# Four key units of the second batch moved into the first batch's weight chain, and its values spread wider

## The chip, the core and the metric

One core of a Trainium2 chip runs the whole kernel. The metric is device microseconds of one execution. TensorE (PE) multiplies and transposes into PSUM, VectorE (DVE), ScalarE (ACT) and GpSimd (POOL) do the rest, and SyncE (SP) issues most of the DMAs from one queue, in order.

## What is computed

Agent attention over four batches of 11,456 tokens of width 128, with 49 agents a batch, and then a mixture of eight experts of which each token goes to one:

```python
a2k = sm(agents, k)              # 49 x 11456, softmax over the keys
agent_v = a2k @ v                # 49 x 128
x = (sm(q, agents) @ agent_v).reshape(B * S, D)
logits = xn @ en.T / tau         # xn, en: rows scaled to length one
expert_idx = np.argmax(logits, axis=1)
out[mask] = gate_w[mask, None] * (np.maximum(x[mask] @ w1[e], 0.0) @ w2[e])
```

## The kernel before

**Units and tiles.** A batch is cut into 12 units of 8 columns of 128 tokens (the last is short), and each unit into two tiles, 23 in all. A *key unit* (`("k", b, u)`) is loaded, transposed, multiplied with the batch's agents (`aT_all`) to 392 columns of scores, copied to SBUF (`s_u`), and taken into a running maximum (`m_run`). After the last, `k_max` makes the maximum over all keys. A *value unit* (`k2_unit`) takes the exponentials of a key unit's scores and multiplies them with the values. `av_chain` folds the sums into `avT`, the 49 agents' values, from which `pick_expert` finds the expert that most tokens of the batch will take, loads its weights (`w1s`, `w2s`), multiplies `avT` with `w1s` (`gp`), orders the hidden units by a key of each (`key`, spread over the partitions by the products `row`, ranked by L739 and L741), gathers the first 256 (`placed`, then `gh`, `gl`; `w2pp`, then `w2p`) and makes a linear remainder (`linp`, `lin`) and a test for tokens that need more (`vm`, `thr`). A *query unit* (`q_unit`) yields the attention weights `tt`, transposed, and then the tiles of the network: `hp`, `hh` and `hl`, `yp`, `ot`, with one store for each tile.

**Two ways for a key unit.** The first batch's go through `k1_f32`: eight 32-bit transposes on TensorE in two halves, one copied out by ScalarE and one by VectorE (`pe_T`), then eight 32-bit products, which the profile shows as 16, with 49 columns. For later batches the odd units do the same. The even ones (`k1_pairs`) are scaled and split into two 16-bit parts (L462, L466, L472), transposed by a DMA on SP's queue (`kT`, L477), and multiplied in 24 16-bit products (L486 to L488).

**Order.** The instructions are written by generators (`spawn`, `yield`) that a loop advances tick by tick: four ticks for each tile, 92 for a batch. A scheduler then orders each engine's queue from a timeline of its own; `in_place(x)` only says that what it encloses comes after `x` on that engine, and `tc.high_priority()` that it goes ahead where it can. In the profile each engine works through its queue in order.

**The stages.** `first()` writes the first batch's keys and values, and then, with nothing of the network to do yet, the chain of `av_chain(0, 0)` and `pick_expert`. TensorE's waits there are filled with products of a tile of zeros (`zero_products`: `ZV` in front of the fold, `ZG` in front of `gp`, `ZA` in front of `row`, `ZB` in front of `placed`). The third and fourth query units (`q_unit(0, 2)`, `q_unit(0, 3)`) are brought up beside it; lists such as `c_last`, `g_last`, `s_last` hold the last instruction of `gp`, of `row` and of the ranking, for `in_place`. After the chain, the first batch's tiles run beside the second batch's keys and values, which `plan()` asks for at fixed ticks: `W_` holds for each batch the shares of a batch at which keys begin and end and values begin and end. The loads go into a ring of `LB` = 10 buffers, in the order in which they are asked for; a load waits until the buffer ten before it has been used.

## Time and profile before

| what | value |
|---|---|
| median of 3 runs | 755.49 us (755.04 to 762.77) |
| the profiled execution | 765.48 us, of which 763.7 us span |
| mean granted TensorE clock | 0.949 |
| busy: TensorE, VectorE, ScalarE, GpSimd | 700.0, 586.5, 468.2, 347.1 us |
| DMA | 125.61 MB, 164 GB/s on the mean |

Busy times are unions over the span, and matmuls are pipelined with modelled ends, so a full TensorE is one that always has something in flight. The clock is a share of 2.4 GHz; 0.50 is the 1.2 GHz level.

### The profile page before, as it was taken

How to read it: one execution, taken by the hardware profiler on the slowest of the kernel's cores; microseconds unless marked ns; L12 is line 12 of the kernel's file. 1: busy time of each engine (PE TensorE's matmuls, PEld its weight loads, DVE VectorE, ACT ScalarE, POOL GpSimd, SP SyncE). 2: the span in 40 equal slices, each digit the busy share in tenths (PEclk: the TensorE clock that was granted, in tenths of full speed). 3: DMA queues.
4: the chain of work that ended last, by engine and by line, in shares of the span. 5: the costliest groups of instructions: out<-in, count | busy, mean ns of one | idle time of the engine just before them, and what ended most of it. 6: DMA issues, size and time to landing. Idle time of an engine off the chain costs nothing. (4 is left out here: it accounts for less than half of the span.)

```text
span 763.7 us, 20762 instructions
## 1 busy us (share of the span) xinstructions
PE 700.0 (92%) x7980; PEld 598.5 (78%) x7980; DVE 586.5 (77%) x1594; ACT 468.2 (61%) x1216; POOL 347.1 (45%) x605
## 2 busy tenths in 40 slices
PE   8998999879997989999999769999999989899996
PEld 7986789768887868778788658887888868777675
DVE  4654898758764898976578789897678799868993
ACT  3354577748663883477567566566656774469841
POOL 5000148236523551676361671547662763866500
PEclk9967899989998989999999879999999999999999
DMA  9935089996854953966795914957563742332321
GB/s 341 282 111 184 12 226 235 242 200 154 217 153 147 291 115 122 269 147 198 181 201 163 262 47 98 285 151 223 131 200 94 219 112 56 104 58 83 128 73 63
DMA packets 167285, 125.61 MB, mean 164 GB/s; under 512 B 87034, under 2 KB 143440, under 8 KB 167186
## 3 DMA queue, kind: packets, MB, share of 16 engines
q1 hardware_dynamic: 153746, 100.59, 52.3%
q10 hardware_dynamic: 13120, 23.47, 8.7%
q8 instruction: 63, 1.03, 0.6%
q14 instruction: 36, 0.29, 0.1%
q0 software_dynamic: 320, 0.23, 0.1%
HBM read 80.26 MB, written 23.79 MB: 136 GB/s over the span
## 5 line engine op out<-in xcount | busy, mean ns | idle before, releaser
L1157 ACT ACTIVATE hh<-hp 128x512 f16<-128x512 f32 (+1 forms) x184 | 106.9, 586 | 65.0 <-PE hp L1154 52.5
L1158 DVE SCALAR_TENSOR_TENSOR hl<-hp,hh 128x512 f16<-128x512 f32 (+1 forms) x184 | 122.4, 667 | 26.2 <-ACT hh L1157 25.4
L1181 PE MATMUL yp<-w2p,hh 128*128 128x128 f16 x720 | 138.6, 221 | 1.8 <-ACT hh L1157 1.6
L1182 PE MATMUL yp<-w2p,hh 128*128 128x128 f16 x720 | 138.8, 221 | 0.0
L1183 PE MATMUL yp<-w2p,hl 128*128 128x128 f16 x720 | 136.1, 221 | 0.9 <-DVE hl L1158 0.9
L1025 ACT ACTIVATE vp<-vp,la 128x320 f32<-128x320 f32 x224 | 112.0, 500 | 31.6 <-PE vp L1022 21.5
L1022 PE MATMUL vp<-vm,tt 128*128 128x320 f16 x360 | 98.5, 301 | 9.5 <-DVE vmin L1027 2.8
L869 PEld LDWEIGHTS sp<-aT_all,fT 128*128 128x128 f32 x720 | 90.1, 198 | 5.4 <-issue 1.6
L869 PE MATMUL sp<-aT_all,fT 128*128 128x49 f32 x720 | 92.1, 278 | 1.1 <-DVE qe L879 1.1
L1181 PEld LDWEIGHTS <-hh 128*128 128x128 f16 x720 | 72.8, 101 | 17.5 <-ACT hh L1157 6.2
L888 POOL TENSOR_TENSOR e<-qe,e 128x392 f16<-128x392 f32 (+1 forms) x46 | 41.4, 901 | 92.5 <-ACT e L887 81.4
L1183 PEld LDWEIGHTS <-hl 128*128 128x128 f16 x720 | 72.0, 100 | 10.4 <-issue 2.2
L1182 PEld LDWEIGHTS <-hh 128*128 128x128 f16 x720 | 71.6, 99 | 5.2
L1027 DVE TENSOR_REDUCE vmin<-vp 128x1 f32<-128x320 f32 (+1 forms) x136 | 64.7, 479 | 13.0 <-PE vp L1022 12.4
L1153 PE MATMUL hp<-tt,gh 128*128 128x512 f16 (+1 forms) x184 | 70.0, 382 | 2.5 <-DVE vmin L1027 1.0
L1154 PE MATMUL hp<-tt,gl 128*128 128x512 f16 (+1 forms) x184 | 69.8, 380 | 0.0
L972 POOL TENSOR_TENSOR nrm<-qq,half 128x16 f32<-128x16 f32 (+2 forms) x28 | 68.5, 2448 | 0.5
L1196 DVE TENSOR_TENSOR ot<-yp,gs 128x512 f32<-128x512 f32 (+1 forms) x92 | 61.4, 669 | 7.4 <-PE yp L1183 6.9
L1172 PE MATMUL yp<-lin,tt 128*128 128x128 f16 x720 | 64.6, 222 | 0.4
L420 DVE COPY fT<-fTp 128x512 f32<-128x512 f32 x68 | 46.2, 679 | 23.4 <-PE fTp L416 23.0
L423 ACT COPY fT<-fTp 128x512 f32<-128x512 f32 (+1 forms) x80 | 44.6, 559 | 30.0 <-PE fTp L416 20.2
L416 PE MATMUL fTp<-ident,qt 128*128 128x128 f32 (+1 forms) x344 | 55.0, 286 | 2.6 <-ACT vp L1025 1.6
(361 smaller groups left out, 1753.5 us busy)
## 6 DMA issues: line engine op xcount, KB each, us to landing
kt<-in_k_dram SPq DMA_DIRECT2D x44, 512.0 KB, 7.1
vt<-in_v_dram SPq DMA_DIRECT2D x44, 512.0 KB, 6.1
out_dram<-ot ACTq DMA_DIRECT2D x88, 256.0 KB, 3.0
qt<-in_q_dram SPq DMA_DIRECT2D x42, 512.0 KB, 5.2
w1s<-in_moe_w_dram SPq DMA_DIRECT2D x9, 512.0 KB, 3.6
w2s<-in_moe_w_dram SPq DMA_DIRECT2D x9, 512.0 KB, 5.5
q<-in_q_dram SPq DMA_DIRECT2D x2, 512.0 KB, 12.0
tt<-e SPq DMA_TRANSPOSE x46, 3.6
```

The lines of the kernel that those rows point to most:

```text
L869: i_ = pe.matmul(out=s[:p, c * A : (c + 1) * A], lhsT=xT[:, c * p : (c + 1) * p], rhs=aT_all[:, b, :], start=True, stop=True)
L972: pool.tensor_tensor(out=nrm, in0=quad, in1=half[:, :n], op=ALU.pow)
L1022: pe.matmul(out=z[:p, :FV], lhsT=tts[b, u][:, c * p : (c + 1) * p], rhs=bt.vm, start=True, stop=True)
L1025: act.activation(z[:p, :FV], z[:p, :FV], AF.Relu, bias=bt.l[:p, at], scale=-1.0, accum_out=bt.vsum[:p, at])
L1027: dve.tensor_reduce(out=bt.vmin[:p, at], in_=z[:p, :FV], axis=AX.X, op=ALU.min)
L1153: pe.matmul(out=hp[:, :m], lhsT=bt.gh[:, fs], rhs=tt, start=True, stop=False)
L1154: pe.matmul(out=hp[:, :m], lhsT=bt.gl[:, fs], rhs=tt, start=False, stop=True)
L1157: h_last[:] = [act.activation(hh[:, :m], hp[:, :m], AF.Relu)]
L1158: dve.scalar_tensor_tensor(out=hl[:, :m], in0=hp[:, :m], scalar=0.0, in1=hh[:, :m], op0=ALU.max, op1=ALU.subtract)
L1181: pe.matmul(out=y, lhsT=hh[:, cs], rhs=wh, start=False, stop=False, skip_group_check=True)
L1182: pe.matmul(out=y, lhsT=hh[:, cs], rhs=wl, start=False, stop=False, skip_group_check=True)
L1183: y_last[:] = [pe.matmul(out=y, lhsT=hl[:, cs], rhs=wh, start=False, stop=last, skip_group_check=True)]
```

## The change

Four key units of the second batch (`NEXT = 4`) are loaded while the first batch's values come free, and worked on in the first batch's chain, all four in 32 bits. Units 0 to 2 are transposed after the transpose in `av_chain` that ends it (`q_last`). The scores of units 0 and 1 and the transposes of unit 3 come after `gp`; the scores of units 2 and 3 come after `row`, and their copies after the ranking. The maxima of units 1 to 3 are taken on VectorE after the copy that makes `w2p`; unit 0's scores become the running maximum by a copy on GpSimd. Zero products in front of `gp` go from 8 to 2, those in front of `row` are left out, and those in front of `placed` go from 18 to 6. The third query unit's transposes come after the scores of unit 3. In the plan the other eight key units take 0 to 0.19 of a batch where twelve took 0 to 0.28, and the values 0.24 to 0.52.

```diff
--- before.py
+++ after.py
@@ -60,12 +60,13 @@
     LEAD = min(4, NU)
     LAG = 5
     HOLD = 2
+    NEXT = 4
     TB = 8
     XB = 3
     LB = 10
     XS = 2
     WARM = 9
-    ZV, ZG, ZA, ZB = 3, 8, 10, 18
+    ZV, ZG, ZB = 3, 2, 6
 
     groups = [[0]]
     while groups[-1][-1] < NU - 1:
@@ -377,6 +378,7 @@
 
     y_last, h_last, p_last, w_last = [], [], [], []
     k_T = {}
+    z_last, q_last = [], []
     a_last, f_last, n_last, c_last, v_last = [], [], [], [], []
     k_last, m_last, d_last, r_last, s_last, g_last = [], [], [], [], [], []
     h_slots = slots(XS)
@@ -415,7 +417,7 @@
                 for c in range(m):
                     pe.transpose(out=tp[:, c * p : (c + 1) * p], in_=src[:p, c0 + c, :], identity=ident[:p, :p])
             dst = xT[:, c0 * p : (c0 + m) * p]
-            if c0 and not both:
+            if (c0 and not both) or both is None:
                 with in_place(floor[0]):
                     dve.tensor_copy(dst, tp[:, : m * p])
             else:
@@ -446,6 +448,57 @@
         run_max(kb, spv, p, n)
         kb.s[u] = st
         kb.k1 += 1
+
+    ahead = {}
+
+    def sure(g):
+
+        try:
+            next(g)
+        except StopIteration as x:
+            return x.value
+        raise AssertionError("no room")
+
+    def ahead_T(u, after, both=False):
+
+        i = sure(take(x_slots))
+        p, n = ushape(u)
+        ahead[u] = i, pe_T(units["k", 1, u], p, n, after, both=both)
+        used("k", 1, u)
+
+    def ahead_s(u, after, psx):
+
+        p, n = ushape(u)
+        s = psx("sp")
+        j, kT = ahead[u]
+        with in_place(after):
+            for c in range(n):
+                i = pe.matmul(out=s[:p, c * A : (c + 1) * A], lhsT=kT[:, c * p : (c + 1) * p], rhs=aT_all[:, 1, :], start=True, stop=True)
+        give(x_slots, j)
+        ahead[u] = s
+        return [i]
+
+    def ahead_copy(u, after):
+
+        kb = blk_of(1, u)
+        p, n = ushape(u)
+        kb.at[u] = sure(take(s_slots))
+        st = wk.tile([P, UJ, A], F32, name="s_u", tag="s_u", bufs=NU)[:p, :n]
+        with in_place(after):
+            act.copy(st, ahead.pop(u)[:p, : n * A].rearrange("p (c a) -> p c a", a=A))
+        if kb.k1 == 0:
+            pool.tensor_copy(kb.m_run[:p, :n, :], st)
+        kb.s[u] = st
+        kb.k1 += 1
+
+    def ahead_max(after):
+
+        kb = blk_of(1, 0)
+        for u in range(1, NEXT):
+            p, n = ushape(u)
+            mr = kb.m_run[:p, :n, :]
+            with in_place(after):
+                dve.tensor_tensor(out=mr, in0=kb.s[u], in1=mr, op=ALU.max)
 
     def k1_pairs(b, u):
 
@@ -592,8 +645,10 @@
         dve.tensor_scalar(bt.sg6, bt.sg, 1e-6, None, ALU.mult)
         yield 4
         s = psx("avsT")
-        pe.transpose(out=s[:A, :D], in_=bt.avT[:, :A], identity=ident)
+        i = pe.transpose(out=s[:A, :D], in_=bt.avT[:, :A], identity=ident)
         act.copy(av_all[:, b, :], s[:A, :D])
+        if b == 0:
+            q_last[:] = [i]
 
     def urgent(g, k):
 
@@ -665,6 +720,12 @@
             i = pe.matmul(out=gp[:, c * A : (c + 1) * A], lhsT=w1s[:, c * P : (c + 1) * P], rhs=bt.avT[:, :A], start=True, stop=True)
         if b == 0:
             c_last[:] = [i]
+            a_ = c_last
+            for u in range(min(2, NEXT)):
+                a_ = ahead_s(u, c_last, pss)
+                ahead_copy(u, ())
+            if NEXT > 3:
+                ahead_T(3, a_)
         s2, i2 = yield from half_scale(ssq, 2, "w1")
         sgw = sm.tile([P, 1], F32, name="sgw", tag="sgw")
         dve.tensor_scalar(sgw, s2, bt.sg, None, ALU.mult)
@@ -721,8 +782,6 @@
         yield g
         for h in range(2):
             t_ = psx("row")
-            if b == 0 and not h:
-                zero_products(t_, ZA, c_last)
             hs = slice(h * 512, h * 512 + 512)
             for c in range(NF // 2):
                 i = pe.matmul(out=t_[:, c * P : (c + 1) * P], lhsT=key[:, h * NF // 2 + c : h * NF // 2 + c + 1].broadcast_to([P, P]),
@@ -730,6 +789,9 @@
             act.copy(row[:, hs], t_)
             if b == 0 and h:
                 g_last[:] = [i]
+                z_last[:] = g_last
+                for u in range(2, NEXT):
+                    z_last[:] = ahead_s(u, g_last, psh if u == 3 else pss)
             yield g
 
         if b > 0:
@@ -742,6 +804,8 @@
             if b == 0:
                 s_last[:] = [i]
             yield g
+        for u in range(2, NEXT) if b == 0 else ():
+            ahead_copy(u, s_last)
         hi = slice(NF // 2, NF)
         dve.tensor_scalar(rank[:, hi], more[:, hi], -0.5, (F - 1) / 2, ALU.mult, ALU.add)
         yield 1
@@ -752,7 +816,7 @@
         def placed(h, w):
             t_ = psx("placed")
             if b == 0 and w == FM and not h:
-                zero_products(t_, ZB, g_last)
+                zero_products(t_, ZB, z_last)
             t_ = t_[:, :w]
             for c in range(NF):
                 pe.matmul(out=t_, lhsT=gt16[:, h, c].rearrange("p h a -> p (h a)"), rhs=sel[:, c, :w],
@@ -854,7 +918,7 @@
         if early:
             xT = pe_T(units["q", b, u], p, n, m_last[u:] if u else k_last, both=True)
         elif lead:
-            xT = pe_T(units["q", b, u], p, n, p_last[:1] if u == 2 else v_last)
+            xT = pe_T(units["q", b, u], p, n, z_last if u == 2 else v_last)
         else:
             xT = pe_T(units["q", b, u], p, n, p_last)
         used("q", b, u)
@@ -1435,7 +1499,6 @@
 
 
 
-    NEXT = 0
     AHEAD = LB - 2
 
     def first():
@@ -1443,7 +1506,7 @@
         X = {"k": k, "v": v, "q": q}
         lead = [ld.tile([P, F], F32, name="q%d" % i, tag="w%ds" % (i + 1), bufs=1).rearrange("p (c d) -> p c d", d=D) for i in range(2)]
         loads = [("k", 0, u) for u in range(LB)] + [("q", 0, u) for u in range(2)] + [None]
-        loads += [("k", 0, u) for u in range(LB, NU)] + [("v", 0, u) for u in range(NU)] + [("q", 0, u) for u in range(2, LEAD)]
+        loads += [("k", 0, u) for u in range(LB, NU)] + [("v", 0, u) for u in range(NU)] + [("q", 0, 2)] + [("k", 1, u) for u in range(NEXT)] + [("q", 0, 3)]
 
         def fetch(n):
             for o in loads[:n]:
@@ -1463,6 +1526,7 @@
 
         asked = []
         k_start(0)
+        k_start(1)
         for u in range(NU):
             if u == 3:
                 spawn(agents16())
@@ -1486,15 +1550,19 @@
             yield 1
         with tc.high_priority():
             now_run(av_chain(0, 0))
-        spawn(q_unit(0, 2, (1, 1, 1, 1, 1)))
         while len(tts) < 2:
             yield 1
         yield 2
+        with tc.high_priority():
+            for u in range(min(3, NEXT)):
+                ahead_T(u, q_last)
         with tc.high_priority():
             while not hasattr(batches[0], "w2p"):
                 next(batches[0].pick)
+        spawn(q_unit(0, 2, (1, 1, 1, 1, 1)))
         yield 2
         spawn(q_unit(0, 3, (1, 1, 1, 1, 1)))
+        ahead_max([batches[0].o_])
         yield from batches[0].pick
 
     S = NT * TICKS
@@ -1505,7 +1573,7 @@
     def plan():
 
 
-        W_ = [(0, 0.28, 0.30, 0.52), (-0.66, 0.12, 0.16, 0.58), (-0.66, 0.12, 0.16, 0.58)]
+        W_ = [(0, 0.19, 0.24, 0.52), (-0.66, 0.12, 0.16, 0.58), (-0.66, 0.12, 0.16, 0.58)]
         kv, qs, at = [], [], -UT * TICKS
         for b in range(1, B):
             k0, k1_, v0, v1 = (S * (b - 1 + x) for x in W_[b - 1])
```

## Rows read from the trace of the kernel before

**Rows 1.** Windows: busy (count) of PE, PEld, DVE, ACT, POOL; clock, DMA share, GB/s.

```profile
97.00:290.00 193.00, 175.48 (x2081) 151.99 (x2081) 149.58 (x359) 131.10 (x325) 94.62 (x154) 0.93 0.80 200
```

**Rows 2.** The same columns for three stretches of the first batch stage.

```profile
95.00:110.00 15.00, 14.99 (x157) 13.41 (x155) 14.92 (x39) 11.19 (x23) 8.25 (x12) 1.00 0.84 212
...
125.00:140.00 15.00, 12.24 (x155) 11.49 (x155) 11.23 (x27) 10.31 (x27) 8.27 (x16) 0.97 1.26 262
...
155.00:170.00 15.00, 9.76 (x114) 8.01 (x113) 7.78 (x16) 6.28 (x18) 7.13 (x10) 0.77 1.01 221
```

**Rows 3.** The timeline of 156 to 172 us; in brackets idle before, releaser.

```profile
164.42 0.22 PE L486 MATMUL sp<-a,kT 128*128 128x49 f16 x1 [5.13 <-DMA kT<-ks]
```

**Rows 4.** TensorE's timeline through the chain.

```profile
65.89 3.57 PE L189 MATMUL gp<-zeros 128*128 128x512 f16 x8 [0.35 <-ACT av_all L596]
...
70.10 1.45 PE L416 MATMUL fTp<-ident,qt 128*128 128x128 f32 x8
...
71.39 0.99 PE L665 MATMUL gp<-avT,w1s 128*128 128x49 f32 x8
...
76.04 4.43 PE L189 MATMUL row<-zeros 128*128 128x512 f16 x10
...
80.26 2.39 PE L728 MATMUL row<-ident,key 128*128 128x128 f32 x16
...
82.97 4.05 PE L189 MATMUL placed<-zeros 128*128 128x512 f16 x18
...
87.23 1.97 PE L869 MATMUL sp<-aT_all,fT 128*128 128x49 f32 x16
...
89.22 1.91 PE L758 MATMUL placed<-sel,gt 128*128 128x256 f16 x16
```

**Rows 5.** ScalarE's timeline in the chain.

```profile
69.22 1.06 ACT L658 ACTIVATE sel<-w1s 128x1024 f16<-128x1024 f32 x1 [2.68 <-DMA w1s<-in_moe_w_dram]
```

**Rows 6.** VectorE's timeline in the chain.

```profile
77.84 0.17 DVE L709 TENSOR_SCALAR nkey<-key 128x8 f32<-128x8 f32 x1
...
94.03 0.68 DVE L800 CAST w2p<-w2pp 128x512 f16<-128x512 f32 x1
```

**Rows 7.** Groups, 95 to 175 us, by form: xcount | busy us, mean ns.

```profile
L439 PE MATMUL sp<-aT_all,fT 128*128 128x49 f32 x80 | 9.8, 274 | 0.0
...
L472 DVE SCALAR_TENSOR_TENSOR ks<-kt,hsc,ks 128x1024 f16<-128x1024 f32 x6 | 8.5, 1415 | 0.0
...
L420 DVE COPY fT<-fTp 128x512 f32<-128x512 f32 x11 | 7.4, 673 | 6.2 <-PE fTp L416 6.0 <-PE sp L439 0.2
...
L462 ACT ACTIVATE ks<-kt 128x1024 f16<-128x1024 f32 x7 | 7.4, 1056 | 3.9 <-DMA kT<-ks 3.9
...
L416 PE MATMUL fTp<-ident,kt 128*128 128x128 f32 x42 | 6.5, 290 | 2.8 <-ACT vp L1025 2.8
...
L486 PE MATMUL sp<-a,kT 128*128 128x49 f16 x48 | 5.0, 191 | 5.1 <-DMA kT<-ks 5.1
...
L406 DVE TENSOR_TENSOR m_run<-s_u,m_run 128x392 f32<-128x392 f32 x6 | 3.9, 652 | 0.3 <-ACT s_u L492 0.3
```

**Rows 8.** Windows, columns as in rows 1: the clock beside what TensorE does.

```profile
26.00:33.00 7.00, 7.00 (x66) 6.97 (x66) 3.43 (x10) 2.76 (x6) 0.23 (x2) 1.00 1.15 287
...
37.00:46.00 9.00, 9.00 (x43) 8.29 (x42) 3.41 (x8) 2.69 (x6) 0.00 (x0) 0.50 0.27 73
...
51.00:60.00 9.00, 9.00 (x159) 8.47 (x154) 4.28 (x10) 4.80 (x9) 0.12 (x1) 1.00 0.54 180
...
65.00:71.00 6.00, 5.56 (x22) 3.09 (x23) 1.44 (x9) 2.78 (x7) 0.00 (x0) 0.50 0.73 222
...
71.00:74.00 3.00, 2.50 (x23) 2.37 (x21) 1.40 (x6) 1.26 (x3) 0.20 (x1) 1.00 0.99 393
```

**Rows 9.** TensorE's timeline where the clock is at 0.50.

```profile
41.88 1.78 PE L869 MATMUL sp<-aT_all,fT 128*128 128x49 f32 x8
...
44.19 1.97 PE L416 MATMUL fTp<-ident,q 128*128 128x128 f32 x8
```


## The prediction

> **What bounds the kernel now.** I read the windows by stage first. The reader is to see there that the run has two kinds of time: a first stretch of 97 us in which the first batch's keys, values and weights are brought up, and four batch stages of which the first takes 193 us, with the tensor engine busy 175.48 of them [rows 1]. Cut finer, the first batch stage starts with the vector engine full (14.92 of 15 us), and later holds two holes of the tensor engine, 12.24 and 9.76 us busy of 15, at a DMA share of 1.26 and 1.01 [rows 2]. The second hole has a name: the product of a key unit waits 5.13 us for its transposing DMA [rows 3]. So the first batch stage is mostly bound by the tensor engine, with the vector engine close behind and with two holes that the DMA queue makes.
>
> Next the tensor engine in order of time through the chain that picks the second weights [rows 4]. It is busy there too, but much of it is products of zeros: eight in front of `gp`, ten in front of `row`, eighteen in front of `placed`. The question is then where these stand in the way already. The weights are there at 69.22, when ScalarE starts to square them [rows 5], but `gp` starts at 71.39, behind zeros and transposes. The key is ready at 77.8, when its negative is taken [rows 6], but `row` starts at 80.26, behind ten zero products of 4.43 us. `placed` starts at 89.22, right where the score products of the third query unit end (87.23 + 1.97). So all three steps of this chain already start when the tensor engine gets free, and whatever the change puts there is on the path.
>
> **The change, part by part.** *Work taken out of the first batch stage.* Units 0 and 2 went by halved 16-bit pairs, 1 and 3 in 32 bits. From the groups of 95 to 175 us [rows 7], a 32-bit unit costs the tensor engine 16 score products at 9.8 / 80 us, which is 1.96, and 8 transposes at 6.5 / 42 us, 1.24: 3.2 us. A pair unit has 24 products of which the eight of L486 take 5.0 / 6 = 0.83 us together with the two lines that run beside them; I take 0.65 to 0.83, so 0.7. Four units: 2 x 3.2 + 2 x 0.7 = 7.8 us. The vector engine loses two subtractions of 1.42 and two maxima of 0.65 for the pair units and about 1.2 each for the others: 6.5 us. ScalarE loses two squarings of 1.06, as many scalings, and the copies. All three engines lose work of one size, so whichever of them is behind at a given moment, the stage is shortened by roughly the same: I take 7.8. The bounds are 0 (something else sets the end of the stage) and 7.8 plus the holes.
>
> *Two transposing DMAs and four loads taken out of the same stage.* The SP queue loses two of the six `kT` transposes. What that is worth I can only bound: nothing, or the whole of the idle time in the two holes, 2.8 + 5.2 = 8.0 us [rows 2]. The named wait of 5.13 us belongs to a late unit that is still there, but it comes at the end of a crowded stretch which now begins with less. I take half of that wait, 2.5 us.
>
> *Values spread over 0.24 to 0.52.* 193 us over 92 ticks are 2.1 us a tick. The first value unit is asked for 0.06 x 92 = 5.5 ticks sooner, the last (0.4967 against 0.5017) half a tick, 1 us. The chain for the second batch hangs on the last one. I take 0, bounds -1 and 0; what hides the earlier start is that values need the maximum over all keys, and these are done sooner as well.
>
> *Transposes of units 0 to 2 in front of `gp`.* Out go six of eight zero products (six eighths of 3.57 = 2.68 us) and the transposes of the third query unit (1.45). In come 24 transposes; this stretch is at clock 0.50 [rows 8], where eight of them took 1.97 [rows 9], so 5.9 us. That is +1.8, and all of it on the path, since `gp` waits for the tensor engine: `gp` at 73.2. PSUM is no limit by the rows: a half unit takes 1.0 us there, its copy out 0.67 (L420), on two engines with little else to do until 69.22.
>
> *Scores of units 0 and 1 and the transposes of unit 3 in front of `row`.* Ten zero products go. In come 2 x 1.96 + 1.24 = 5.2 us if the clock is up, 2 x 3.56 + 1.97 = 9.1 if it is down [rows 9]. The key came 6.4 us behind the start of `gp`, so it comes at 79.6. `gp` takes some 2.1 (two lots of 0.99 and a sum), to 75.3; with 0.6 for the second sum of squares the tensor engine is free at 81.1, or at 85.0. Against 80.26 that is +0.8, or +4.7. I take +0.8 (the zero products which now overshoot the key by 2.3 us pay for most of it) and keep the other. Two score copies of at most 0.7 each on ScalarE could slip ahead of the squares on which the key hangs: 0 to +1.4; I take 0, as they become ready later.
>
> *Scores of units 2 and 3 in front of `placed`.* Twelve of eighteen zero products go (two thirds of 4.05 = 2.7), 3.9 us come. The third query unit's transposes, which now wait for these scores, may come ahead of `placed` or behind: 0 or +1.2. So +1.2, or +2.4; the first tile of `sel` sets a floor some 0.3 below. I take +1.2. The two copies behind the last ranking step fit in ScalarE's gap.
>
> *Three maxima after the w2p copy.* 3 x 0.65 = 1.95 us on the vector engine straight behind 94.03 [rows 6], where it is full. Queued behind them are the tiles for `vm`, the second half of `lin` and the first `hl`, for which the first products of the stage wait. The relief of 6.5 us comes in the same 20 us. I take +1, bounds 0 and 2.
>
> *Loads.* Four key loads go out on SP between the third and the fourth query unit's, as the values' buffers come free, with a DMA share of 0.54 between 51 and 60 us [rows 8]. Behind them on SP stands the load of the picked weights, which were there at 69.22; 2 MB at the 393 GB/s of 71 to 74 us are 5.3 us, so they are through before it. Cost 0; if that cover failed, at most 2 us of the weights' landing.
>
> The sum: -7.8 - 2.5 + 0.8 + 1.2 + 1 = -7.3 us. The profiled execution took 765.48 us, 763.7 of span and 1.8 around it, 10 above the median of the runs shown; the terms are differences, so I set them against the median: 755.49 - 7.3 = 748.2. By the unknowns of this case alone 743 (the whole 5.13 and a free chain) to 756 (nothing for the wait, and the dearer end of each term of the chain).
>
> **The clock, and a rule that speaks against the change.** From 37 to 46 us the tensor engine is busy 9.00 of 9.00 us with nothing but 32-bit transposes, score products and a few small ones, and the clock stays at 0.50, the 1.2 GHz level. From 26 to 33 us the same mix runs at 1.00 throughout [rows 8]. So such work keeps a clock that is up and, here, does not bring it up. It came up around 71 us behind zero products: 65 to 71 is at 0.50, 71 to 74 at 1.00. The change replaces most of these very products.
> The Trainium skill, TensorE: Matmul & The Clock Gate (Part 4: PE-mode transpose), says that transposes do not count as busy for the clock in the way that products do; the rows from 37 to 46 agree, those from 26 to 33 do not show it. By that rule the clock would stay down through the chain, which is the first rival below.
>
> **The rivals.** *The clock stays down from 65 us to the first wide products.* `gp` is then 1.8 + 1.5 late (16 products at 3.56 against some 2.0) and ends at 76.8; scores, transposes and the sum take 9.7, `row` starts at 86.5, +6.2, and itself takes about 1.5 more; behind it 2 x 3.56 + 6 x 0.44 = 9.8 stand where 6.0 stood, +3.8: 11.5 in all, 17 with the third query unit ahead of `placed`. With the 7.8 of the stage and no more: 759 to 765. It ends slower from the point at which the chain's loss passes the 7.8. For it speak the 9 us at 0.50; against it that the clock came up at 71 with transposes making up the last part of that stretch, and that two and six zero products are left.
> *The gain does not come.* The end of the stage may be set by the second batch's chain, by its own weight load and by DMA, whatever the tensor engine is spared: then only the chain's +3 is left: 755 to 759. Against it speak 175 busy of 193 us.
> *Both holes close.* Then 7.8 + 8.0 less the chain's +3: 743, or 739 with `row` at its key (79.6, 0.7 sooner than now) and nothing lost behind it. For it: both lie where keys and values are loaded together.
> *The change does not do what it says.* The program's order is made by a scheduler; it may put scores and transposes behind `row`, where they cost the chain nothing and fill no wait: 746. I count it with the forecast.
>
> **How the numbers follow.** Forecast 0.48, clock down 0.20, no gain 0.14, holes closed 0.18. One per cent is 7.6 us, about what this kernel's own runs (755.04 to 762.77) leave to be told from no change. Half of the forecast's case and nearly all of the last lie below 747.9: faster 0.41. Over 763.0 lies some 0.12 of the first rival and 0.04 elsewhere: slower 0.16. The rest, 0.43, is within 1%. The range takes in the closed holes and most of the slow clock: 739 to 763.
>
> **What would show it.** Right: no zero products between `gp` and `row`; `row` within 1.5 us of 80.26; `placed` by 92; the clock back at 1.00 before 82; only four `kT` transposes for the second batch; the first batch's last tile some 7 us sooner after the first. Wrong: a clock of 0.50 from 65 to past 85 us, `placed` after 98, or the same wait of some 5 us for a `kT` with the stage no shorter. A new wait of `gp` for the weights' DMA would show that the moved loads collide.

## The result

The changed kernel takes 757.6 us (median of 20 runs, 746.63 to 769.65); the kernel before took 763.6 in the 20 runs beside them. The ratio between undisturbed runs (those within 1.5% of their kernel's fastest) is 0.990, 95% interval 0.986 to 0.994; the ratio of the two medians is 0.992. So the gain is about 1%, right at the line between "faster" and "no change". In per cent the sum of the prediction is met (755.49 to 748.2 is 0.990). In microseconds it is 9 too low, and 8 of these are the base: the kernel before takes 763.6 beside it (762.4 over the 107 runs beside the experiments), not the 755.49 of the first three.

The two profiled executions (765.48 and 762.39 us), cut at the same five marks: 20 us, the fold of the first batch, the copy of `w2p`, the first output tile of the second batch, that of the third, and the end. Windows of the kernel before (columns as in [rows 1]):

```profile
20.00:60.50 40.50, 39.35 (x385) 36.90 (x385) 21.51 (x63) 17.40 (x36) 2.21 (x10) 0.83 0.67 179
60.50:94.00 33.50, 29.62 (x205) 21.50 (x204) 21.59 (x72) 16.91 (x32) 1.98 (x6) 0.80 0.31 111
94.00:301.40 207.40, 189.53 (x2216) 164.16 (x2215) 163.68 (x409) 137.93 (x338) 95.83 (x158) 0.93 0.77 191
301.40:484.80 183.40, 167.63 (x2007) 145.16 (x2006) 147.90 (x390) 118.13 (x309) 91.35 (x155) 0.95 0.69 179
484.80:763.70 278.90, 256.32 (x3046) 215.75 (x3045) 222.54 (x638) 171.16 (x491) 144.79 (x238) 0.99 0.47 127
```

and of the changed kernel:

```profile
20.00:61.80 41.80, 40.65 (x398) 38.21 (x396) 22.63 (x64) 18.15 (x38) 2.32 (x11) 0.84 0.74 207
61.80:95.10 33.30, 30.54 (x269) 27.99 (x268) 24.49 (x79) 19.92 (x39) 2.82 (x7) 0.90 0.42 149
95.10:292.00 196.90, 183.22 (x2148) 158.71 (x2147) 157.59 (x400) 131.50 (x329) 95.60 (x157) 0.95 0.69 175
292.00:476.10 184.10, 171.56 (x2000) 148.78 (x1999) 148.56 (x386) 119.29 (x308) 91.35 (x155) 0.92 0.70 187
476.10:760.20 284.10, 259.90 (x3035) 218.95 (x3031) 224.14 (x638) 171.42 (x491) 144.63 (x238) 0.97 0.45 124
```

As measured, the first batch stage (third line) is 10.5 us shorter: TensorE is busy 6.3 us less in it and idle 4.2 us less. The forecast for it was 9.3, which is 7.8 and 2.5 less 1 for the maxima. The chain (second line) is no longer than before, though 64 more matmuls stand in it; its clock is higher. The last line is 5.2 longer, at a lower clock.

A lower clock stretches the work: the 16 products `row` take 2.02 us at 1.00 in the changed kernel's chain below, and 3.75 at 0.50 in e1's. So I read every length a second time with the clock taken out: length times mean granted clock, which is the length less half of the time at 1.2 GHz. Where TensorE idles at the low clock this takes out too much; it is a yardstick, not a time. For whole runs I use the run's time less its span times (1 - clock), and call it the time at full clock. Over all runs it is 726.0 for the kernel before and 722.5 (within 1.2) for the changed one. The changed kernel's times lie 23 us apart, with 49 to 94 us at the low clock; the standard deviation of its times at full clock is 2.7. So most of the spread of one and the same kernel is its clock.

The same two executions by this yardstick (with the clock as the trace has it, before rounding):

| stretch | before, at full clock | changed, at full clock | difference | as measured |
|---|---|---|---|---|
| up to the fold | 33.7 | 35.0 | +1.3 | +1.3 |
| chain | 26.7 | 29.9 | +3.2 | -0.2 |
| first batch stage | 193.7 | 186.7 | -7.0 | -10.5 |
| second batch stage | 174.9 | 168.7 | -6.2 | +0.7 |
| the rest | 275.6 | 276.4 | +0.8 | +5.2 |

The two readings differ where it matters. As measured, the gain is all in the first batch stage, and the last line gives half of it back. At full clock the stage gives 7.0, the last line next to nothing (its 5.2 us are the clock of this execution), and 6.2 us come from the second batch's stage, where the change takes out no work. One trace of each kernel can't settle it; the many traces of the experiments say more.

The chain in the changed kernel, TensorE's timeline:

```profile
67.17 1.01 PE L190 MATMUL gp<-zeros 128*128 128x512 f16 x2 [0.35 <-ACT av_all L649]
68.08 2.77 PE L418 MATMUL fTp<-ident,kt 128*128 128x128 f32 x12
71.39 1.99 PE L720 MATMUL gp<-avT,w1s 128*128 128x49 f32 x12
...
74.56 0.29 PE L418 MATMUL fTp<-ident,kt 128*128 128x128 f32 x1
74.69 0.32 PE L476 MATMUL sp<-aT_all,fT 128*128 128x49 f32 x2
...
77.67 1.07 PE L476 MATMUL sp<-aT_all,fT 128*128 128x49 f32 x8
78.58 1.06 PE L418 MATMUL fTp<-ident,kt 128*128 128x128 f32 x8
80.59 2.02 PE L787 MATMUL row<-ident,key 128*128 128x128 f32 x16 [0.95 <-DVE key L768]
82.45 3.67 PE L476 MATMUL sp<-aT_all,fT 128*128 128x49 f32 x32
85.95 1.46 PE L190 MATMUL placed<-zeros 128*128 128x512 f16 x6
```

`gp` starts where it did [rows 4], although the fold came 1.3 us later, because only twelve of the 24 transposes of units 0 to 2 stand in front of it. They take 0.23 us each, the price at the low clock (at 1.00 the same twelve take 1.48 us in e2's trace). The other twelve come behind `gp`, most of them one by one between the scores of units 0 and 1. `row` now waits 0.95 us for its key and not for TensorE: the hole is filled with keys, and in this trace is just large enough. TensorE's clock in the stretch in front of `row`, before and then in the changed kernel:

```profile
75.00:81.00 6.00, 5.41 (x16) 2.84 (x17) 4.88 (x19) 2.86 (x5) 0.00 (x0) 0.50 0.32 127
```

```profile
75.00:81.00 6.00, 5.05 (x50) 4.84 (x49) 4.89 (x20) 5.26 (x10) 0.51 (x1) 1.00 0.78 313
```

Before, the ten zero products in front of `row` ran at 0.50 and took 4.43 us [rows 4]; the scores and transposes that stand there now run at 1.00. By these lengths the chain gets back by the clock what the keys cost it; why the clock is up there now, no run isolates. The longest waits of TensorE in the stage behind it (total, times, longest):

```profile
PE yp L1245 <- ACT hh L1221: 3.0, 2, 2.7
PE gp L720 <- DMA w1s<-in_moe_w_dram: 2.3, 1, 2.3
PE sp L539 <- DMA kT<-ks: 2.0, 1, 2.0
```

The wait for `kT` is 2.0 us where it was 5.13 [rows 3]. That need not be the units' doing: the longest such wait in the stage is 3.8 us in f1's trace and 2.1 in f2's, where all units are in the stage and only the order differs, and 5.1 in e2's, where four are out of it.

### The profile page after: what moved, and what is told of

Same layout as the page of the kernel before. It is cut to its first block, busy times and chain, and to the rows that moved or that the text cites. A ratio compares the mean times of both kernels' runs of the same rounds, so it can differ in the third digit from the quotient of the medians.

```text
span 760.2 us, 20692 instructions
## 1 busy us (share of the span) xinstructions
PE 702.8 (92%) x7952; PEld 606.4 (80%) x7952; DVE 585.6 (77%) x1587; ACT 466.2 (61%) x1212; POOL 347.6 (46%) x606
## 3 DMA queue, kind: packets, MB, share of 16 engines
HBM read 80.26 MB, written 23.79 MB: 137 GB/s over the span
## 5 line engine op out<-in xcount | busy, mean ns | idle before, releaser
L1091 DVE TENSOR_REDUCE vmin<-vp 128x1 f32<-128x320 f32 (+1 forms) x136 | 65.0, 479 | 16.2 <-PE vp L1086 15.7
L1236 PEld LDWEIGHTS <-tt 128*128 128x128 f16 x720 | 50.6, 102 | 7.6 <-issue 3.4
```

The lines of the kernel that those rows point to most:

```text
L1236: pe.matmul(out=yp[:p, c, :], lhsT=tc_, rhs=bt.lin[:, h], start=(c == 0 and h == 0), stop=False, skip_group_check=True)
```

## The experiments

Every kernel was run in five rounds beside the kernel before. "Low" is the mean time at 1.2 GHz in a run, "full" the time at full clock, with its 95% interval (from both, four runs far above their kernel's others are left out: 798.84 us of the kernel before, 1653.67 of e3, 771.51 of e12, 797.38 of e13). "Stage" and "behind" are from the one profiled execution of each: the first batch stage, and all that follows it, as measured and, in brackets, at full clock.

| run | ratio, 95% | low, us | full, us | stage, us | behind, us |
|---|---|---|---|---|---|
| before | 1 | 73 | 726.0 ± 0.6 | 207.4 (193.7) | 462.3 (450.4) |
| changed | 0.990, 0.986 to 0.994 | 70 | 722.5 ± 1.2 | 196.9 (186.7) | 468.2 (445.2) |
| e1 old spread | 0.990, 0.986 to 0.994 | 61 | 724.7 ± 1.2 | 195.4 (183.5) | 464.3 (455.1) |
| e2 zeros back | 1.000, 0.996 to 1.004 | 63 | 729.3 ± 1.6 | 207.9 (192.5) | 463.5 (445.6) |
| e3 no zeros | 1.013, 1.006 to 1.021 | 74 | 733.2 ± 1.9 | 197.1 (190.3) | 479.5 (457.0) |
| e4 spared stage | 0.979, 0.974 to 0.985 | 57 | 716.1 ± 2.3 | 191.2 (187.8) | 461.4 (440.9) |
| e5 before, few zeros | 0.999, 0.994 to 1.004 | 70 | 726.0 ± 1.6 | 205.9 (192.3) | 460.6 (453.5) |
| e6 two units | 1.028, 1.020 to 1.037 | 102 | 729.6 ± 2.5 | 213.8 (191.6) | 469.0 (451.7) |
| e8 before, 32 bits | 0.999, 0.995 to 1.003 | 47 | 738.6 ± 0.8 | 209.3 (202.5) | 461.2 (454.1) |
| e9 third query sooner | 0.990, 0.985 to 0.995 | 70 | 723.5 ± 1.1 | 197.6 (189.1) | 465.8 (446.9) |
| e10 maxima later | 0.995, 0.991 to 0.999 | 70 | 724.7 ± 1.9 | 199.4 (190.9) | 461.9 (446.9) |
| e12 spared, with loads | 0.984, 0.978 to 0.991 | 71 | 710.8 ± 1.7 | 191.5 (184.6) | 458.3 (441.1) |
| e13 bare chain | 1.005, 1.001 to 1.009 | 84 | 722.4 ± 1.3 | 201.7 (191.4) | 466.4 (448.1) |
| e14 no loads | 0.997, 0.992 to 1.001 | 73 | 722.1 ± 1.7 | 194.0 (188.8) | 468.6 (447.0) |
| f1 before, respread | 1.005, 1.001 to 1.009 | 67 | 731.1 ± 1.2 | 207.3 (195.3) | 464.4 (455.0) |
| f2 before, respread | 1.001, 0.997 to 1.005 | 60 | 730.3 ± 1.4 | 213.8 (196.7) | 457.3 (451.6) |
| p2 two units, old spread | 0.991, 0.986 to 0.995 | 66 | 721.1 ± 1.9 | 199.3 (190.8) | 462.7 (445.6) |
| p3 three units | 1.006, 1.002 to 1.010 | 67 | 733.2 ± 2.2 | 203.3 (193.1) | 472.0 (455.7) |

**One part of the change at a time.** e1 takes back the values' spread, e2 puts the zero products back beside the keys, e3 takes the last of them out from in front of `gp` and `placed`.

```
e1:  W_ = [(0, 0.19, 0.30, 0.52), ...     # 0.24 in the changed kernel
e2:  ZV, ZG, ZA, ZB = 3, 8, 10, 18        # and zero_products(t_, ZA, c_last) ahead of row
e3:  ZV, ZG, ZB = 3, 0, 0
```

> The changed kernel with the values spread over 0.30 to 0.52 again; all else of the change stays. My prediction put the wider spread at 0: then this stays at some 0.990 of the kernel before (0.985 to 0.995). Rival: the gain is the second batch's weight chain coming sooner. In the changed kernel its weights were asked for at 222 us instead of 239, and the second batch's first tile came 9.4 us sooner. If the spread does this, half or more of the gain goes with it: 0.995 to 1.000, and the weights are asked for past 230 us.

> The changed kernel with the zero products of the kernel before put back: eight, ten and eighteen. My steps price these at 2.7, 4.4 and 2.7 us of the tensor engine on the chain's path, less what the waits hide: row starts 3 to 4 us later than in the changed kernel, placed 4 to 6, and the ratio is 0.995 to 0.998. Rival, the clock needs the zero products: the clock in the chain comes up sooner, and the ratio is 0.985 to 0.990.

> The changed kernel without any zero products in front of gp and placed. If transposes and scores are enough for the clock, as the changed kernel's own trace suggests (it came up at 72.4 us and stayed up through the chain), nothing changes: 0.987 to 0.993, and the clock is at 1.00 from 75 us on. Rival, the clock stays down from 65 us without them: row starts 5 us or more later, placed 10, and the ratio is 1.000 to 1.008.

The spread is worth nothing that the ratio shows (e1, 0.990 again); at full clock e1 lies 2.2 us above the changed kernel (within 1.7). Its rival falls: the second batch's weights were asked for at 232.5 us, as late as the rival would have it, and the gain stayed.

With the zeros back the gain is gone. Full goes up by 729.3 - 722.5 = 6.8 us, and 28 more zero products at 1.46 / 6 us each (the last line of the chain's timeline above) are 6.8 too. But e2's trace doesn't have the 6.8 us in the chain. Its chain and stage, and TensorE's timeline in the chain:

```profile
61.70:95.80 34.10, 32.69 (x280) 26.72 (x279) 24.25 (x78) 19.66 (x38) 3.85 (x10) 0.95 0.39 140
95.80:303.70 207.90, 189.74 (x2161) 162.81 (x2161) 159.83 (x398) 131.26 (x328) 93.68 (x155) 0.93 0.67 166
```

```profile
69.86 1.48 PE L418 MATMUL fTp<-ident,kt 128*128 128x128 f32 x12
...
81.14 2.00 PE L789 MATMUL row<-ident,key 128*128 128x128 f32 x16
...
90.80 1.25 PE L824 MATMUL placed<-sel,gt 128*128 128x256 f16 x10
```

The chain is 0.8 us longer than the changed kernel's, 2.5 at full clock. Counted from the fold, `row` starts 0.6 us later and `placed` 1.3, where I had expected 3 to 4 and 4 to 6. Most of the loss lies in the stage behind it, which is 11 us longer, 6 at full clock, with no zero product in it. So the two 6.8 agree by chance as far as this trace tells, and a price of the zero products isn't shown.

e3 loses 10.7 us at full clock, but not in the chain, which is 31.9 us long in its trace; it comes behind the second batch. In that trace the clock is at 1.00 from 65 to 88 us, so it was up, as expected, with keys in place of these zero products; this is one execution.

e1's trace shows something else. It caught the first rival in one execution: the clock stayed down through the chain, with TensorE busy.

```profile
56.00:100.10 44.10, 41.69 (x268) 38.35 (x268) 24.58 (x80) 20.19 (x39) 2.42 (x7) 0.65 0.32 113
62.00:93.00 31.00, 30.03 (x145) 27.65 (x143) 15.65 (x47) 16.23 (x27) 0.74 (x2) 0.50 0.39 136
```

```profile
80.17 3.75 PE L787 MATMUL row<-ident,key 128*128 128x128 f32 x16 [0.95 <-DVE key L768]
83.72 6.90 PE L476 MATMUL sp<-aT_all,fT 128*128 128x49 f32 x32
90.42 2.73 PE L190 MATMUL placed<-zeros 128*128 128x512 f16 x6
```

The chain's instructions are those of the changed kernel, 268 of them against 269; the chain takes 44.1 us and not the 33.5 of the kernel before, so +10.6, where the rival had priced 11.5. e9's trace has it too (46.3 us at clock 0.63); those of the changed kernel, e10 and e14, with the same chain, don't, nor do those of e2 and e3. By the Trainium skill, TensorE: Matmul & The Clock Gate (Part 4: PE-mode transpose), transposes do not count as busy for the clock the way products do. The first 18 of these 31 us, transposes among products, fit it. But from 80.17 to 93 us TensorE does products alone, without a gap, and is still at 0.50; and 62 to 93 us in e10, most of it the same chain, are at 0.92. So the rule alone does not settle which of the two happens.

**The stage without the chain.** e4 is the kernel before with the chain as it was; the four units are neither loaded, transposed nor multiplied, and their scores are set to zero on GpSimd. e12 is e4 with the loads, which nothing reads.

```
e4:   NEXT = 4;  W_ = [(0, 0.19, 0.24, 0.52), ...
      ...
      for u in range(NEXT):               # ahead of q_unit(0, 2)
          kb.at[u] = next_slot()
          kb.s[u] = wk.tile([P, UJ, A], F32, name="s_u", tag="s_u", bufs=NU)
          pool.memset(kb.s[u], 0.0)
          ...
e12:  loads += ... [("q", 0, 2)] + [("k", 1, u) for u in range(NEXT)] + [("q", 0, 3)]
```

> The kernel before, with the changed plan, in which the scores of the second batch's key units 0 to 3 are set to zero on GpSimd and not computed at all: neither loaded nor transposed nor multiplied. So the output differs for the second batch. The chain is that of the kernel before. It shows what the stage is spared when the chain pays nothing. My terms: 7.8 + 2.5 us, 0.986, and the changed kernel lies some 3 us above it (0.990). Rival, no gain in the stage itself: 0.995 to 1.000. Rival, both holes close: 0.979.

> The spared stage (the kernel before with the scores of the second batch's first four key units set to zero, neither transposed nor multiplied), but with the four units' loads issued early, ahead of the last query unit's, as the changed kernel issues them; nothing reads them. Theory (the 8 us between the spared stage and the changed kernel are the keys' work in the chain, and the loads are free): 0.976 to 0.983, the spared stage's 0.979. Rival (the loads are what costs, ahead of the fourth query unit and in the ring of tiles): 0.987 to 0.992.

Sparing the stage is worth 2.1% (15.7 us of 764), of which 9.9 are at full clock; the rest is clock. The 9.9 look like the 10.3 forecast, but they don't lie where the forecast had them. From the chain on, e4's trace reads:

```profile
55.10:86.30 31.20, 27.31 (x206) 19.99 (x206) 21.64 (x73) 16.66 (x32) 2.02 (x6) 0.89 0.34 119
86.30:277.50 191.20, 176.24 (x2143) 152.45 (x2142) 157.55 (x399) 130.34 (x327) 95.11 (x158) 0.98 0.72 185
277.50:461.30 183.80, 169.81 (x1983) 147.04 (x1982) 146.04 (x386) 119.12 (x308) 90.82 (x155) 0.92 0.73 185
461.30:738.90 277.60, 257.08 (x3048) 217.44 (x3046) 222.74 (x638) 171.23 (x491) 144.79 (x238) 0.98 0.46 127
```

At full clock the stage is 187.8 us, 5.9 below the kernel before, and what follows it is 9.5 below (440.9 against 450.4), though no work was taken out there. The loads cost nothing that shows (e12: 0.984, within e4's interval; at full clock 710.8, which is 5.3 below e4, though e12 only does more).

So 6.4 us at full clock (722.5 - 716.1; 11.7 against e12) and some of the clock are lost between e4 and the changed kernel. In the traces e4's chain is 27.8 at full clock, 2.1 less than the changed kernel's 29.9; its stage is no shorter (187.8 against 186.7); and behind the stage it is 4.3 less (440.9 against 445.2). So a third of the 6.4 is the chain, and the rest stands in the later batches.

**What takes the rest?** Four suspects: the zeros, the wait for `kT`, the third query unit's transposing DMA, the maxima.

```
e5 (before):   ZV, ZG, ZA, ZB = 3, 2, 0, 6
e8 (before):   return u % 2 == 0 and (b > 1 or u > 3)      # by_pairs
e9 (changed):  third = q_unit(0, 2, (1, 1, 1, 1, 1))       # its transposes wait for c_last
               with tc.high_priority():
                   for _ in range(4): next(third)
e10 (changed): yield from batches[0].pick
               ahead_max(())                               # was ahead of it
```

> The kernel before, with only its zero products cut to those of the changed kernel (2, none and 6 in place of 8, 10 and 18), and no keys in the holes that they leave. Theory (the holes were free, and the 26 products that go were only cover): the chain from the fold to w2p stays at 33.5 us within 1, and the ratio is 0.997 to 1.003. Rival (the products held TensorE's clock up): the clock is at 0.50 over most of the chain, which comes to 38 to 44 us, and the ratio is 1.006 to 1.014. Third (the zero products stood in the way of the query units behind them): the third query unit's transposing DMA goes earlier against w2p, and the ratio is 0.985 to 0.995.

> The kernel before, with units 0 and 2 of the second batch taken in 32 bits like the odd ones: their two transposing DMAs go, and TensorE's work on them grows by 2 x (3.2 - 0.7) = 5 us. Theory (the stage of the first batch's queries waits for those DMAs: 5.1 us at 159 us and more behind it, so that half of the 15.7 us that a spared stage gives are waits and not work): the wait at 159 us goes, TensorE's added work takes its place, and the ratio is 0.994 to 1.002. Rival (the stage is bound by TensorE's work alone, and the wait comes up elsewhere): +5 us, 1.005 to 1.009.

> The changed kernel, with the first four steps of the third query unit (its transposes, copies and the transposing DMA) put ahead in the order, right behind the step that gives w2p, and its transposes free to go from the gradient's product on. Theory (of the 8 us that the changed kernel lies above the spared stage, several are the third query unit's transposing DMA and the loads queued behind it on SyncE's queue, which go 2.5 us behind w2p where the spared stage has them at w2p): the DMA goes at w2p or before, and the ratio to the kernel before is 0.982 to 0.987. Rival (the 8 us are the chain's own work on TensorE and VectorE): 0.988 to 0.994, or above it where the transposes now stand in front of the row's scores.

> The changed kernel, with the three running maxima of the keys put behind the end of the pick and not at its last steps. Theory (they cost VectorE 1 us or less there, in a stage that TensorE bounds): 0.987 to 0.992, the changed kernel's own 0.990 within what can be measured. Rival (they stand ahead of the first query units' copies on VectorE, and carry a good part of the 8 us): 0.982 to 0.986.

e5: without keys the zeros cost nothing, as they stand in holes: the chain is 33.4 us without them. e9 and e10 don't gain: neither the query unit's place nor the maxima are it, and the theory that had named the DMA falls; the DMA of e9 goes at the time of `w2p`, and the stage is 197.6 us and not 196.9. e10 came out at 0.995, above both of its ranges. e8 came out as expected, but the step behind it is only half right. The wait falls to 3.3 us, not to nothing, and the full time grows by 12.6 us, not by 5 (in the trace 8.8 of it are in the stage); what keeps the time level is 26 us less at the low clock.

**The chain without the stage.** e13 is the changed kernel with all its rearrangement, but no keys are loaded, transposed or multiplied for the four units (scores zero); e14 has all the work, but its transposes read a query tile, and no keys are loaded.

```
e13:  def ahead_T(u, after, both=False): return
      def ahead_s(u, after, psx): return after
      ahead_copy: pool.memset(st, 0.0) for act.copy(st, ...)
e14:  ahead[u] = i, pe_T(units["q", 0, 2], p, n, after, both=both)
both: ("k", 1, u) out of loads
```

> The changed kernel with its zero products, its late third query unit and its running maxima, but the four units' loads, transposes, products and score copies left out and their scores set to zero on GpSimd. Theory (the keys' work in the chain costs the 8 us): 0.976 to 0.983, as the spared stage in the chain of before. Rival (what costs is the rearrangement: the third query unit moved behind the scores, the maxima, the fewer zero products): 0.986 to 0.992. Between them, 0.983 to 0.986: both.

> The changed kernel with all its work, but the four units' loads left out: the transposes read the third query unit's tile in their place, so that the scores are not the keys'. Theory (work costs, loads are free): 0.986 to 0.993, as the changed kernel. Rival (the loads cost): 0.976 to 0.983.

e14 is the changed kernel to 0.4 us at full clock: loads are free there too. Its ratio, 0.997, is above the theory's 0.993 all the same, with an interval that reaches below it. e13 fell outside everything expected: with less work than e4 or the changed kernel it is slower than before. Part is clock. Its empty chain runs at 0.74, and it has 84 us at the low clock in a run, 14 more than the changed kernel:

```profile
63.70:96.20 32.50, 24.32 (x178) 20.84 (x178) 21.46 (x73) 16.68 (x32) 1.92 (x6) 0.74 0.35 130
```

The other part is at full clock (722.4, 6.3 above e4), behind the chain: its second and third stages are of another make than those of before (170.2 and 296.2 us where those are 183.4 and 278.9). That turned the question: how much does the order alone move?

**The number of units, and the order alone.** The planner interleaves all later work by due times, so an edit here can change the order of thousands of later instructions. f1 and f2 are the kernel before with its work untouched and two due fractions moved; e6 and p2 have two units in the chain and differ in these fractions alone; p3 has three.

```
f1 (before):  W_ = [(0, 0.26, 0.28, 0.52), ...     # 0.28, 0.30
f2 (before):  W_ = [(0, 0.24, 0.27, 0.52), ...
e6 (changed): NEXT = 2;  W_ = [(0, 0.235, 0.27, 0.52), ...
p2 (changed): NEXT = 2;  W_ = [(0, 0.28, 0.30, 0.52), ...
p3 (changed): NEXT = 3;  W_ = [(0, 0.21, 0.24, 0.52), ...
```

> The changed kernel with two of the units in the chain in place of four, the values spread over 0.27 to 0.52. Theory (each spared unit gives the stage 15.7 / 4 = 3.9 us, and the chain takes 8 / 4 = 2 back for each, in proportion): half of the change's gain, 0.994 to 0.997. Rival (the first two units, which stand in the hole ahead of the row, are free, and the two behind the row carry the cost): 7.8 us, 0.988 to 0.991. Third (the gain needs all four, since the transposing DMAs' wait moves on to the next unit): 0.998 to 1.002.

> The kernel before with no key in the chain; only the two numbers over which the second batch's keys and values are spread are shifted a little (0.26 and 0.28 for 0.28 and 0.30), so that the same work is interleaved in another order. Theory (the order alone moves the time by a per cent either way, through the later batches and TensorE's clock): the ratio lies anywhere in 0.990 to 1.015, and the time less half of the time at the low clock (726.1 us for the kernel before) within 5 us of it. Rival (the order is worth nothing, and every difference between the runs so far is the edit's own): 0.997 to 1.003, and 725 to 727 us.

> As the run before it, shifted twice as far (0.24 and 0.27). Theory (order alone): anywhere in 0.990 to 1.015, and not in line with the smaller shift. Rival (an earlier spread as such is better or worse): the same sign as the smaller shift, and more of it.

> The changed kernel with two units in the chain and the spread of the kernel before (0.28, 0.30). Theory (the 2.8% of the other kernel with two units are its order and its clock, not the number of units): 0.990 to 1.010, well under 1.028. Rival (two units are worse than none or four, since the chain's holes are left half empty and the clock falls): 1.020 to 1.035 again.

> The changed kernel with three units in the chain (spread 0.21, 0.24). Theory (order): 0.985 to 1.010. Rival (by number: none 1.000, two 1.028, four 0.990): between two and four, 1.005 to 1.015. By the units' work alone, three quarters of the changed kernel's gain, it would be 0.9925.

Order alone costs f1 0.5% (0.1 to 0.9) and both f1 and f2 4 to 5 us at full clock, though f2, with the larger shift, gets it back by the clock. e6 and p2, the same units in the chain, lie 3.8% apart. Two units with the old spread give what four give. So the time does not go by the number of units. Windows of f1:

```profile
302.90:468.50 165.60, 158.25 (x1944) 135.60 (x1944) 139.57 (x373) 113.67 (x301) 87.46 (x144) 1.00 0.68 179
468.50:767.40 298.90, 270.62 (x3103) 224.55 (x3099) 233.48 (x653) 175.53 (x498) 148.24 (x249) 0.97 0.46 129
```

It is the make of e13: the second stage 18 us shorter than before, the rest 20 longer. The traces of e1, e5, e6, e8 and f2 have it too, e3 and p3 its long last part; the others have the make of before. And e6's first batch stage, 213.8 us, has the clock further down than p2's; at full clock the two stages are alike (191.6 and 190.8). First e6's windows, then p2's:

```profile
225.00:245.00 20.00, 19.31 (x138) 17.45 (x137) 8.38 (x28) 9.50 (x21) 1.64 (x3) 0.66 0.78 219
265.00:281.00 16.00, 12.39 (x87) 9.76 (x87) 15.41 (x40) 10.87 (x32) 9.44 (x20) 0.57 0.09 34
```

```profile
225.00:245.00 20.00, 14.81 (x164) 13.57 (x162) 10.86 (x32) 7.56 (x21) 6.70 (x10) 0.86 0.35 113
265.00:281.00 16.00, 14.42 (x163) 12.36 (x162) 15.82 (x37) 16.00 (x40) 10.32 (x19) 1.00 0.41 123
```

Of the 26.5 us between the means of e6 and p2 (780.5 and 754.0), 18 are 36 us more at the low clock, and 8.5 are at full clock.

At full clock the first batch stage goes by the units more than by the order. The kernel before, e5, f1 and f2 have all twelve key units of the second batch in it, in four orders: 205.9 to 213.8 us, 192.3 to 196.7 at full clock. The ten kernels with four units out of it have 191.2 to 207.9 us, 183.5 to 192.5 at full clock. The means lie 11 us apart, 6 at full clock. Behind the stage all kernels are asked for the same work, and it takes 457 to 480 us, 441 to 457 at full clock.

## Why the prediction came out as it did

Two steps failed: the base of the sum, and the end of the account at the first batch stage. The terms for the stage had the right sign and, as measured, the right size; those for the chain lie between the two readings of it.

- *The base*: "I set them against the median: 755.49". This step failed; it is 8 of the 9 us by which 748.2 was too low. The kernel before takes 763.6 beside the changed one. Three runs of a kernel whose runs mostly lie between 752 and 774 were too few; the profiled execution (765.48) had said so. From 763.6 the sum gives 756.3, and 757.6 was measured, but that is in part luck, by the next point.
- *The later batches*, not in the sum at all: this step failed too. I ended the account where the first batch stage ends, and put what follows at nothing without a reason. With the same work it takes 441 to 457 us at full clock by the order; f1 shows that a mere reordering moves the time by 0.5%, and e6 against p2, in part in the first batch stage, by 3.8%. This is as large as the whole forecast. In the pair of traces the part behind the stage is 5.9 us longer as measured and 5.2 shorter at full clock.
- *The stage*, -7.8 and -2.5, and +1 for the maxima in it: the sign is shown, as the stage is shorter in nearly every order that was run. By -11 as measured the -9.3 fits; at full clock the traces give -6. The step "whichever of them is behind, the stage is shortened by roughly the same" was not tried engine by engine. Half of the pair's 10.5 us is not in the first batch's tiles at all: from the last of them to the second batch's first tile it is 12.1 us before and 7.2 in the changed kernel, whose second weights are asked for 17 us sooner. The term for the `kT` wait isn't shown: it shrank by 3.1, and nearly as much in f2, by order alone.
- *The chain*, +0.8 and +1.2: -0.2 as measured and +3.2 at full clock in the pair; over the traces, five chains with the keys are 28.7 to 31.0 at full clock and six of the old make 26.7 to 27.9, so some +2.5. `row` came at 80.59 (forecast within 1.5 of 80.26), `placed` at 89.63 (by 92), the clock was back at 1.00 at 72.4 (before 82). `gp` was forecast at 73.2, behind 24 transposes, and came at 71.39, behind twelve. And the sum took the ten zero products' 4.43 us as it found them, at the clock of 0.50; e2's ten take 2.32 at the higher clock.
- *Loads and the values' spread*, 0: e12 and e14 show no cost of the loads, and e1 none of the spread beyond some 2 us.
- *The clock stays down*, a rival at 0.20 and 759 to 765: right as a mechanism and in its price for the chain (10.6 for 11.5). It is not in every execution: two of the five traces with this chain have it, none of the six with the old one, and e1 is at 0.990 in spite of it. The row from which the prediction read that such work doesn't bring the clock up, 37 to 46 us at 0.50, is at 0.57 in the changed kernel's trace and at 1.00 in those of e1 and e9, whose edits concern later work.
- *The chances*: a sum of -7.3 with a line at 7.6 was cut into 0.43 and 0.41, with "within 1%" as the likeliest. The gain lies on that line (0.990 or 0.992), so that neither was wrong.

So the change gains about 1%, which is what its terms add up to. That four units out of the stage make it shorter is shown. But f1 and e6 keep me from calling the whole gain theirs: the interval says that this program is faster, not that the four units made it so, since the order that came with them is worth as much. The kernels that differ from the changed one in a detail and do its work (e1, e9, e10, e14) lie at 0.990 to 0.997 and 722.1 to 724.7 at full clock, the old work in three other orders (e5, f1, f2) at 0.999 to 1.005 and 726.0 to 731.1, which speaks for the units; e2 and e3, also with four units, at 1.000 and 1.013, speak against it. What e4 and e12 show, with 1.6 to 2.1%, is what the units' absence gives in that order. Why the later batches take more in one order than in another stays open, and no run here keeps their order fixed while it takes the units away. Of the kernels that do the whole work, none beats the changed one beyond its interval.

## What to carry to other kernels

Where a planner lays out the work, run the kernel before with a due time moved a little, and nothing else: its spread is the smallest difference that an edit can be credited with. Split each time into the part at the low clock and the rest before you compare, run by run; the rest is steady to a few microseconds where the times are 20 apart. And when a whole run's difference equals a price, look in the trace whether it lies where the price says: the zero products' 6.8 us and e4's 9.9 both matched, and neither lay there.

## What the runs showed of the hardware

Two things I had not expected. TensorE was busy 30.03 of 31 us at 1.2 GHz in e1, first with 32-bit transposes among products and then with 12.83 us of products alone, while the same chain ran at 0.90 in the changed kernel's trace; what decides between the two no run here shows. And more work can cost no time: e8 has 12.6 us more at full clock and 26 us less at the low clock, and its time is that of the kernel before.
